# Attention then a two-layer block on one core: layer steps over 36 slots a batch, none in the slots that turn a k

## The chip, the cores and the metric

The kernel runs on one core of a Trainium2 chip. A core has a matrix engine (TensorE), three other compute engines (VectorE, ScalarE, GpSimd), and 16 DMA engines, which run side by side and are ordered by semaphores. TensorE writes into PSUM; the other engines bring results from there to SBUF. The metric is the device time in microseconds of one execution, the median of three runs for the kernel before. Less is better.

## The reference

Batched attention with a threshold (8 batches, 8 heads, 576 positions, 64 wide), whose output is the input of two layers with g = h - tanh(h) in between:

```python
scores = scale * np.matmul(q, k.transpose(0, 1, 3, 2))
thresh = np.max(scores, axis=-1, keepdims=True) - tau
scores = np.where(scores >= thresh, scores, -1000000000.0)
scores = scores - np.max(scores, axis=-1, keepdims=True)
attn = np.exp(scores)
attn = attn / (np.sum(attn, axis=-1, keepdims=True) + 1e-09)
x = np.matmul(attn, v)          # heads side by side: 4608 tokens x 512
h = x @ w_in                    # 512 x 2048
g = h - np.tanh(h)
return g @ w_out                # 2048 x 512
```

## The kernel before

The attention is cut into 32 pairs of heads (four a batch) of nine tiles of 128 queries each, 288 tiles in all. One program loop goes through **slots** s; slot s computes the scores of tile s + 8, the `Prelu` of tile s + 5, the `Exp` of tile s, the product with v of tile s - 2, and the preparation of later pairs. Tiles come in twos: z of two tiles is transposed together (by a DMA from pair 6 on, on TensorE before), so `Exp` and the product with v stand in every second slot. An instruction stream per engine follows the order of the loop, so what a slot contains on one engine is done in that order.

The pools (the number is how many buffers a tag has):

```python
    z_pool = pool("z", 4)
    zt_pool = pool("zt", 6)
    p_pool = pool("p", 3)
    o_pool = pool("o", 2)
    wt_pool = pool("wt", 4)
    g_pool = pool("g", 2)
    t_pool = pool("t", 3)
    y_pool = pool("y", 2)
    x_pool = pool("x", 2)
    ps_big = pool("ps_big", 2, space=PSUM)
    ps_o = pool("ps_o", 1, space=PSUM)
    ps_h = pool("ps_h", 2, space=PSUM)
    ps_y = pool("ps_y", 1, space=PSUM)
```

The scores of a tile: four matmuls, the main 512 columns and the other 64, once with k and once with kS, a copy of k whose halves are swapped. VectorE then scales and takes the row maximum in one instruction (L341):

```python
        else:
            lhs = qT[:, (5 * hh + t) * P : (5 * hh + t + 1) * P]
            for n, kk in enumerate((kT, kS)):
                for dst, src in ((main, MAIN[hh]), (rem, REM[hh])):
                    nc.tensor.matmul(
                        out=ps[:, dst], lhsT=lhs, rhs=kk[:, src],
                        start=(n == 0), stop=(n == 1),
                    )
        sc = sc_pool.tile([P, S], F32, name="sc")
        if kind(i) == "B":
            mx = mxs[i] = mxs.pop(i - 1)
        else:
            mx = mxs[i] = mx3[i // 2 % len(mx3)]
        c = int(kind(i) == "B")
        nc.vector.tensor_scalar(
            out=sc, in0=ps[:, lo : lo + S], scalar1=SC, scalar2=None,
            op0=ALU.mult, op1=ALU.max, accum_out=mx[:, c : c + 1],
        )
        scs[i] = sc
```

The `Prelu` on ScalarE (L368) makes z from it, with a DMA transpose (L375) behind each second one; `Exp` (L404) makes the weights pT, and nine matmuls (L425, L432) multiply them with v:

```python
        nc.scalar.activation(
            out=z, in_=sc, func=ACT.Prelu, bias=nb, scale=1.0, alpha=STEEP
        )
        if on_pe(i):
            zts[i] = zt
        elif kind(i) == "B":
            zts[i] = zt_pool.tile([P, TPP, P], BF16, name="zT")
            nc.sync.dma_start_transpose(out=zts[i], in_=zt)
...
        else:
            n += off
            pt = p_pool.tile([P, TPP * P], FP16, name="pT")
            nc.scalar.activation(
                out=pt[:, 0 : n * P], in_=zts.pop(i)[:, 0:n, :], func=ACT.Exp
            )
...
        nc.tensor.matmul(
            out=po[:, t - 1 : t + 1, :], lhsT=pt[:, 4 * P : 5 * P],
            rhs=vb[:, hh, 4:6, :], start=True, stop=False, skip_group_check=True,
        )
        for n in range(8):
            ab, c = divmod(n, 4)
            blk = 5 * ab + c
            nc.tensor.matmul(
                out=po[:, t - 1 + ab, :], lhsT=pt[:, blk * P : (blk + 1) * P],
                rhs=vb[:, hh, c, :], start=False, stop=(n == 7), skip_group_check=True,
            )
```

To **turn** a k: nine transposes on TensorE, a copy on VectorE (L263), and two on GpSimd for the swapped copy kS (L269). q is turned in the same way, or by a DMA:

```python
    def turn(p, t):
        hl = hls.pop((p, t))
        if t == "q" and q_by_dma(p):
            m = mats[p, t] = qk_pool.tile([P, W], FP16, name=f"{t}T", tag=t)
            nc.sync.dma_start_transpose(
                out=m.rearrange("p (c r) -> p c r", c=TPP),
                in_=hl.rearrange("p c a d -> p (c a d)"),
            )
            return
        ps = ps_big.tile([P, W], FP16, name=f"ps_{t}", tag="big")
        for c in range(TPP):
            turn_chunk(
                ps[:, c * P : (c + 1) * P], c, hl[:, c, :, :].rearrange("p a d -> p (a d)")
            )
        m = qk_pool.tile([P, W], FP16, name=f"{t}T", tag=t)
        nc.vector.tensor_copy(out=m, in_=ps)
        mats[p, t] = m
        if t == "k":
            sw = qk_pool.tile([P, W], FP16, name="kS", tag="ks")
            for lo, hi in ((0, D), (D, 0)):
                o, i = sw[lo : lo + D, :], m[hi : hi + D, :]
                nc.gpsimd.tensor_copy(out=o, in_=i)
            mats[p, "ks"] = sw
```

`emit_x` transposes a pair's attention output for the layers; it runs at the fourth or fifth slot of the next pair and takes its PSUM buffer from `ps_h`:

```python
    def emit_x(p):
        o = osb.pop(p)
        pf = ps_h.tile([P, 320], F32, name="psX", tag="h")
        ps = pf[:, 0:256].bitcast(BF16)
        for t in range(4):
            nc.tensor.matmul(
                out=ps[:, t * P : (t + 1) * P],
                lhsT=o[:, t, :, :].rearrange("p a d -> p (a d)"),
                rhs=ident_bf, is_transpose=True, start=True, stop=True,
            )

        nc.tensor.matmul(
            out=pf[:, 256:320], lhsT=o[:, 4, :, :].rearrange("p a d -> p (a d)"),
            rhs=fold, start=True, stop=True,
        )
        b = p // HPAIR
        if p % HPAIR == 0:
            xs[b] = x_pool.tile([P, DM_C, MB], BF16, name="xT")
        nc.vector.tensor_copy(out=xs[b][:, p % HPAIR, :], in_=ps[:, 0:512])
        nc.vector.tensor_copy(out=xR[:, p % HPAIR, b, :], in_=pf[:, 256:320])
```

A **layer step** is one of two: an h step (`hidden`, four matmuls of 512 columns, then `Tanh` on ScalarE and the subtraction on VectorE in the following slot), or a y step (a quarter of `project`, four matmuls of 512 columns; after four quarters VectorE copies y out and a DMA stores it):

```python
    def hidden(m, n, ps):
        if n == 0:
            gs[m] = g_pool.tile([P, DF_C, MB], BF16, name="g")
        for c in range(DM_C):
            nc.tensor.matmul(
                out=ps, lhsT=w_in_sb[:, c, n * P : (n + 1) * P],
                rhs=xs[m][:, c, :] if m < B else xR[:, c, :, :],
                start=(c == 0), stop=(c == DM_C - 1),
            )
        halves.append((m, n, ps))

    halves, ths = [], []

    def bend():
        while halves:
            m, n, ps = halves.pop(0)
            th = t_pool.tile([P, MB], F32, name="th")
            nc.scalar.activation(out=th, in_=ps, func=ACT.Tanh)
            ths.append((m, n, ps, th))

    def shrink():
        while ths:
            m, n, ps, th = ths.pop(0)
            nc.vector.scalar_tensor_tensor(
                out=gs[m][:, n, :], in0=th, scalar=-1.0, in1=ps,
                op0=ALU.mult, op1=ALU.add,
            )

    def project(m, ms, part, ps, last, cols=slice(0, d_model)):
        for n in range(4 * part, 4 * part + 4):
            nc.tensor.matmul(
                out=ps, lhsT=gs[m][:, n, ms * P : (ms + 1) * P],
                rhs=w_out_sb[:, n, cols], start=(n == 0), stop=(n == DF_C - 1),
            )
        if part == 3:
            nc_ = cols.stop - cols.start
            yo = y_pool.tile(
                [P, nc_], F32, name="yo", tag="yo" if nc_ == d_model else f"yo{int(last)}",
                bufs=2 if nc_ == d_model else 1,
            )
            if last:
                nc.scalar.copy(out=yo, in_=ps)
            else:
                nc.vector.tensor_copy(out=yo, in_=ps)
...
        def h_step(n):
            if tail and n % 2:
                ps = ps_big.tile([P, MB], F32, name="psHt", tag="big")
            else:
                ps = ps_h.tile([P, MB], F32, name="psH", tag="h")
            hidden(m, n, ps)

        def y_step(m, ms, part):
            if part == 0:

                odd = tail and (m, ms) > (B - 2, 1) and ms % 2 == 0
                pl, tag = (ps_o, "o") if odd else (ps_y, "y")
                ys[m, ms] = pl.tile([P, d_model], F32, name="psY", tag=tag), odd
            ps, odd = ys[m, ms]
            project(m, ms, part, ps, odd)
```

The steps of stage m are put in an order, h and y by turns; a y step needs the h steps that it reads. A middle stage has 16 h steps and 16 y steps (13 of the batch before, 3 of its own), the first stage 16 and 3:

```python
        now = quarters(m - 1)[EARLY(m - 1) :] if m > 0 else []
        if m < NMB - 1:
            now += quarters(m)[: EARLY(m)]
        else:
            now += quarters(m)[:12]
        n = 16 + len(now)


        ahead = n - max(0, EARLY(m) - 3) - LAST if m < NMB - 1 else n - 9 - LAST
        steps, at, i = [], [], 0

        def ready(y):
            last = 4 * y[2] + 3
            return y[0] < m or len(at) > (last if m else 15) and at[last] + 2 < i

        while now or len(at) < 16:
            if len(at) < 16 and (
                not now or not ready(now[0]) or len(at) * ahead <= i * 16
            ) and not (m == B - 1 and i < FIRST):
                steps.append(lambda a=len(at): h_step(a))
                at.append(i)
            elif ready(now[0]):
                steps.append(lambda y=now.pop(0): y_step(*y))
            else:
                steps.append(lambda: None)
            i += 1
```

Stage m runs beside the attention of batch m + 1. The slot in which the preparation of a pair falls is set in `plan`: `first` is the slot in which the pair's first scores are computed, `d` is how many slots earlier a step comes.

```python
    plan = {}
    for p in range(1, NPAIR):
        first = TPP * p - AHEAD
        for d, f in PREP[3 if p == 1 else 0 :]:
            d -= p == 1 and d in (3, 5)
            if d in (7, 8) and q_by_dma(p):
                d = d + 2
            if p in (2, 4):
                d = {8: 9, 7: 8, 5: 6}.get(d, d)
            elif d == 5 and p >= 5:
                d = 6 if p % 2 else 3
            plan.setdefault(first - d, []).append(lambda p=p, f=f: f(p))
        d = 7 if q_by_dma(p) else 3 - (p == 1 or p >= 5)
        d = 4 if p in (2, 4) else d
        plan.setdefault(first - d, []).append(lambda p=p: turn(p, "q"))
```

The loop, with the spreading of the layer steps. At slot j = 2 + LAG = 4 of a batch's first pair the steps of a stage are made, and `share` of them is due in each slot that follows:

```python
    for s in range(-AHEAD, NTILE + LAG + 3):
        p, j = divmod(max(s, 0), TPP)
        if 0 <= s < NTILE and j == 2 + LAG and p % HPAIR == 0 and p >= HPAIR:
            assert not todo
            todo = layers(stage, False)
            share = len(todo) / (HPAIR * TPP - 2 - LAG)
            done, stage = 0.0, stage + 1
        if s == NTILE:
            todo = layers(stage, True)
            share, done, stage = 1, 0.0, stage + 1
        if 0 <= s + AHEAD - 1 < NTILE:
            shift(s + AHEAD - 1)
        if 0 <= s + AHEAD < NTILE:
            scores(s + AHEAD)
        if s == 1 - AHEAD:
            for t in ("k", "q", "ks"):
                turn_first(t, 1)
        for i in kinks.pop(s, []):
            kink(i)
        bend()
        for i in wts.pop(s, []):
            weights(i)
        if 0 <= s < NTILE + FIRST:
            if todo:
                done += share
                if s < NTILE and j == TPP - 1 and p % HPAIR == HPAIR - 1:
                    done = 1e9
                while todo and done >= 1:
                    todo.pop(0)()
                    done -= 1
        if s == 0:
            nc.vector.tensor_tensor(
                out=fold, in0=ident_bf[:, 0:64], in1=ident_bf[:, 64:P], op=ALU.add
            )
        shrink()
        for store in stores[:-1]:
            store()
        del stores[:-1]
        for i in atts.pop(s, []):
            pp, jj = divmod(i, TPP)
            if i < NTILE:
                attend(i)
                odd = pp % 2
                if jj == 3 + odd:
                    norm(pp, 0)
                elif odd and jj in (0, 8):
                    norm(pp - (jj == 0), 1)
            if pp and jj == 1 + pp % 2:
                emit_x(pp - 1)
        for step in plan.pop(s, []):
            step()
```

Of the kernel before, what the change touches and what calls it, by code (L numbers as in the profile page):

```python
# [18 lines left out]
def kernel(  # L19
# [26 lines left out]
    HPAIR = H // 2  # L46
    NPAIR = B * HPAIR
# [4 lines left out]
    TPP = 9  # L52
    NTILE = NPAIR * TPP
# [9 lines left out]
    AHEAD = 8  # L63
    LDK = 16
    MASK = 5
    LAG = 2
# [177 lines left out]
    def q_by_dma(p):  # L244

        return p >= 2 * HPAIR and p % 4 != 0
# [25 lines left out]
    def turn_first(t, part):  # L272

        hl = hls[0, t[0]]
        c0, c1 = ((0, 5), (5, TPP))[part]
        pl, tag = (ps_y, "y") if t == "ks" else (ps_h, "h")
        ps = pl.tile([P, 5 * P], FP16, name=f"ps1_{t}", tag=tag)
        for c in range(c0, c1):
            o = ps[:, (c - c0) * P : (c - c0 + 1) * P]
            if t == "ks":  # L280
                for a in range(2):
                    turn_chunk(o[64 * a : 64 * a + 64, :], c, hl[:, c, 1 - a, :])
            else:
                turn_chunk(o, c, hl[:, c, :, :].rearrange("p a d -> p (a d)"))
        if part == 0:
            mats[0, t] = qk_pool.tile([P, W], FP16, name=f"{t}T", tag=t)
        dst, n = mats[0, t][:, c0 * P : c1 * P], (c1 - c0) * P
        if part == 1 or t == "q":
            nc.scalar.copy(out=dst, in_=ps[:, 0:n])
        else:  # L290
            nc.vector.tensor_copy(out=dst, in_=ps[:, 0:n])
# [16 lines left out]
    def scores(i):  # L308
        p, hh, t = place(i)
        qT, kT, kS = mats[p, "q"], mats[p, "k"], mats[p, "ks"]  # L310
        ps = ps_big.tile([P, 1024], F32, name="psS", tag="big")
        main, rem, lo = slice(0, 512), slice(512, 576), 0
        if kind(i) == "B":
            main, rem, lo = slice(512, 1024), slice(448, 512), 448
        if hh is None:
            qrem = REM
            if q_by_dma(p):
                qrem = (slice(512, 640, 2), slice(513, 640, 2))
            for n, kk in enumerate((kT, kS)):
                for dst, srcs in ((main, MAIN), (rem, REM)):  # L320
                    for hh in range(2):
                        nc.tensor.matmul(
                            out=ps[64 * hh : 64 * hh + 64, dst],
                            lhsT=qT[:, qrem[hh]], rhs=kk[:, srcs[hh]],
# [22 lines that stand above are left out]
    def shift(i):  # L347

        if kind(i) == "A":
            return  # L350
        mx = mxs.pop(i)
        nb = st_pool.tile([P, 9], F32, name="nb", tag="nb")
        nc.vector.tensor_scalar(  # L353
            out=nb.rearrange("p (a b) -> p a b", b=3)[:, :, 0:2],
            in0=mx.rearrange("p (a b) -> p a b", b=4)[:, :, 0:3],
            scalar1=-1.0, scalar2=tau, op0=ALU.mult, op1=ALU.add,
        )
        nbs[i - 1], nbs[i] = nb[:, 0:1], nb[:, 1:2]

    def kink(i):  # L360
        sc, nb = scs.pop(i), nbs.pop(i)
        if kind(i) == "B":
            zt = zs.pop(i - 1)
            z = zt[:, S:W]
        else:
            zt = zs[i] = z_pool.tile([P, W], BF16, name="z")
            z = zt[:, 0:S]
# [8 lines that stand above are left out]
# [131 lines left out]
# [14 lines that stand above are left out]
# [109 lines left out]
    def w_cast():  # L630
        flat, wt, i, cols = loaded.pop(0)
        nc.gpsimd.tensor_copy(out=flat[:, i * cols : (i + 1) * cols], in_=wt)
# [26 lines left out]
# [13 lines that stand above are left out]
# [16 lines left out]
    todo, stage = [], 0  # L688
# [4 lines left out]
            plan.setdefault(-AHEAD, []).extend(plan.pop(at))  # L693


    kinks, wts, atts = {}, {}, {}
    for i in range(NTILE + 3):
        at = i - 4 if i < HPAIR * TPP else i
# [4 lines left out]
    for s in range(-AHEAD, NTILE + LAG + 3):  # L703
        p, j = divmod(max(s, 0), TPP)
        if 0 <= s < NTILE and j == 2 + LAG and p % HPAIR == 0 and p >= HPAIR:
            assert not todo
            todo = layers(stage, False)
            share = len(todo) / (HPAIR * TPP - 2 - LAG)
            done, stage = 0.0, stage + 1
        if s == NTILE:  # L710
            todo = layers(stage, True)
# [11 lines that stand above are left out]
        for i in wts.pop(s, []):  # L723
            weights(i)
        if 0 <= s < NTILE + FIRST:
            if todo:
                done += share
                if s < NTILE and j == TPP - 1 and p % HPAIR == HPAIR - 1:
                    done = 1e9
                while todo and done >= 1:  # L730
                    todo.pop(0)()
# [22 lines that stand above are left out]
        if s + AHEAD in cast_when:  # L754
            w_cast()
        if s + AHEAD in load_when:
            w_load(next(pieces))
# [54 lines left out]
```

## Time and profile before

| what | value |
|---|---|
| time, median of three runs | 533.57 us (533.13 to 533.61) |
| span of the profiled execution | 532.0 us |
| busy: TensorE, VectorE, ScalarE, GpSimd | 96%, 79%, 82%, 55% |
| the eight batches of attention, from the first score reduction of tile 8 to that of tile 287 | 16.53 to 449.46 us |
| the tail: the rest of the layers | 449.46 to 532.0 us |
| DMA: transposes of z, from issue to landing | 3.5 us, 117 of them |

How to read it: a busy share is an average over the whole span. The kernel has a start, eight batches and a tail, so the batches are looked at one by one, by windows. A matmul's record lasts longer than the time after which the next one starts, because matmuls are pipelined, so that a difference of two starts says what a piece of work costs TensorE, and the length of one record does not. In a line of the timeline, the first number is the start, the second the length of what is merged in the line, and the count at the end says how many instructions are merged; square brackets give the idle time before it and what ended that. "L341" is line 341 of the kernel.

### The profile page before, as it was taken

The page shows a single profiled execution, that of the slowest core. Times are in us where ns is not written, and L with a number is a line of the kernel's source. Part 1 is how long each engine was busy: PE and PEld are TensorE (multiplying, and loading weights), DVE is VectorE, ACT ScalarE, POOL GpSimd, SP SyncE. Part 2 cuts the span into 40 slices and gives each one's busy share as a digit, 9 for nine tenths or more (in the row PEclk, how much of TensorE's full clock was granted, in tenths as well). Part 3 has the DMA queues.
Part 4 walks back from the last instruction along what each step waited for, and adds up shares of the span by engine and source line. Part 5 has one row for each costly group of instructions (what it writes and reads, how often), then busy time and mean ns, then how long its engine had stood idle before and what let it go on. Part 6 is the DMA issues. An engine that isn't in the chain of part 4 may idle for free.

```text
span 532.0 us, 12716 instructions
## 1 busy us (share of the span) xinstructions
PE 509.2 (96%) x4606; PEld 287.6 (54%) x4606; DVE 421.0 (79%) x1179; ACT 435.8 (82%) x617; POOL 290.1 (55%) x390
## 2 busy tenths in 40 slices
PE   8999899988999999999999999999999999999996
PEld 4666566544555555555555555555555555444444
DVE  5899879996888988898889988898889887554440
ACT  5999899988898989898898989898989899543330
POOL 8999989683746657475727574666657530000000
PEclk9999999998999999999999999999999999999999
DMA  7843659979897999789898899999979996400113
GB/s 212 252 133 114 217 186 184 167 160 197 170 209 140 190 184 217 173 179 202 186 197 186 191 188 199 171 185 199 214 160 185 195 149 110 105 33 28 39 41 80
DMA packets 208607, 86.79 MB, mean 163 GB/s; under 512 B 176160, under 2 KB 200992, under 8 KB 208544
## 3 DMA queue, kind: packets, MB, share of 16 engines
q1 hardware_dynamic: 207952, 85.56, 76.0%
q8 instruction: 36, 0.59, 0.5%
q10 hardware_dynamic: 592, 0.43, 0.3%
q14 instruction: 27, 0.22, 0.1%
HBM read 36.70 MB, written 9.44 MB: 87 GB/s over the span
## 4 chain that ended last, share of the span: by engine, by line
PE 35%; issue 20%; POOL 19%; ACT 9%; DMA 8%; DVE 6%; SPq 2%; POOLq 0%; ACTq 0%; DVEq 0%
PE psY L524 12%; PE psH L498 9%; PE psS L331 6%; POOL kS L269 5%; DMA vraw<-in_v_dram 4%; ACT z L368 3%; ACT pT L396 3%; PE psHt L498 3%; DMA kraw<-in_k_dram 3%; POOL khl L193 3%; POOL vb L221 2%; POOL qhl L193 2%; ACT th L511 1%; POOL qhl L192 1%; PE psO L432 1%
## 5 line engine op out<-in xcount | busy, mean ns | idle before, releaser
L341 DVE TENSOR_SCALAR_CACHE_REDUCE sc<-psS 128x576 f32<-128x576 f32 x288 | 214.2, 753 | 39.8 <-PE psS L331 25.9
L368 ACT ACTIVATE z<-sc,nb 128x576 bf16<-128x576 f32 x288 | 216.4, 772 | 22.2 <-DVE nb L353 20.3
L524 PE MATMUL psY<-w_out_sb,g 128*128 128x512 bf16 (+1 forms) x592 | 145.9, 373 | 0.8 <-DVE yo L537 0.8
L404 ACT ACTIVATE pT<-zT 128x1152 f16<-128x1152 bf16 x117 | 135.2, 1156 | 13.4 <-DMA zT<-z 13.2
L269 POOL COPY kS<-kT 64x1152 f16<-64x1152 f16 x62 | 70.9, 1144 | 125.9 <-DVE nb L353 124.4
L498 PE MATMUL psH<-xT,w_in_sb 128*128 128x512 bf16 x480 | 124.1, 381 | 2.6 <-DVE g L517 2.5
L331 PEld LDWEIGHTS <-qT 128*128 128x128 f16 x1024 | 74.8, 98 | 62.3 <-issue 8.4
L331 PE MATMUL psS<-kT,qT 128*128 128x512 f16 (+1 forms) x512 | 104.6, 286 | 3.2 <-DVE sc L341 1.2
L517 DVE SCALAR_TENSOR_TENSOR g<-th,psH 128x512 bf16<-128x512 f32 x128 | 87.6, 684 | 20.9 <-ACT th L511 20.4
L331 PE MATMUL psS<-kS,qT 128*128 128x512 f16 x496 | 101.6, 286 | 1.7 <-POOL kS L269 1.6
L511 ACT ACTIVATE th<-psH 128x512 f32<-128x512 f32 x128 | 74.8, 585 | 22.4 <-PE psH L498 21.8
L524 PEld LDWEIGHTS <-g 128*128 128x128 bf16 x592 | 51.0, 98 | 56.9 <-issue 2.4
L498 PEld LDWEIGHTS <-w_in_sb 128*128 128x128 bf16 x576 | 49.4, 98 | 57.9 <-issue 6.0
L432 PE MATMUL psO<-vb,pT 128*128 128x65 bf16 x1024 | 53.5, 194 | 0.0
L432 PEld LDWEIGHTS <-pT 128*128 128x128 f16 x1024 | 44.4, 98 | 9.7
L193 POOL TENSOR_TENSOR qhl<-qraw,qhl 128x576 f16<-128x576 f32 x31 | 39.7, 1281 | 2.6
L193 POOL TENSOR_TENSOR khl<-kraw,khl 128x576 f16<-128x576 f32 x31 | 39.7, 1281 | 2.6
L396 ACT ACTIVATE pT<-psZ 128x512 f16<-128x512 bf16 (+1 forms) x54 | 35.2, 655 | 3.9 <-PE psZ L387 3.5
L537 DVE COPY yo<-psY 128x512 f32<-128x512 f32 (+1 forms) x31 | 21.2, 682 | 14.1 <-PE psY L524 12.4
L425 PE MATMUL psO<-vb,pT 128*128 128x130 bf16 x128 | 28.3, 221 | 3.3 <-ACT pT L404 2.7
L458 DVE TENSOR_TENSOR osb<-psO,rc 128x256 bf16<-128x256 f32 x64 | 27.2, 424 | 2.2
L263 DVE COPY kT<-ps_k 128x1152 f16<-128x1152 f16 x31 | 23.3, 753 | 4.1 <-PE ps_k L240 4.1
(79 smaller groups left out, 508.8 us busy)
## 6 DMA issues: line engine op xcount, KB each, us to landing
vraw<-in_v_dram SPq DMA_DIRECT2D x32, 256.0 KB, 4.0
out_dram<-yo SPq DMA_DIRECT2D x32, 256.0 KB, 2.8
kraw<-in_k_dram SPq DMA_DIRECT2D x31, 256.0 KB, 3.2
qraw<-in_q_dram SPq DMA_DIRECT2D x31, 256.0 KB, 3.4
wt<-in_moe_w_in_dram SPq DMA_DIRECT2D x8, 512.0 KB, 4.6
wt<-in_moe_w_out_dram SPq DMA_DIRECT2D x8, 512.0 KB, 3.9
zT<-z SPq DMA_TRANSPOSE x117, 3.5
qraw<-in_q_dram SPq DMA_DIRECT2D x32, 32.0 KB, 3.3
```

The source lines that it names most:

```text
L193: nc.gpsimd.tensor_tensor(out=hl[:, :, 1, :], in0=x, in1=hl[:, :, 0, :], op=ALU.subtract)
L269: nc.gpsimd.tensor_copy(out=o, in_=i)
L331: nc.tensor.matmul(out=ps[:, dst], lhsT=lhs, rhs=kk[:, src], start=(n == 0), stop=(n == 1),)
L341: nc.vector.tensor_scalar(out=sc, in0=ps[:, lo : lo + S], scalar1=SC, scalar2=None, op0=ALU.mult, op1=ALU.max, accum_out=mx[:, c : c + 1],)
L368: nc.scalar.activation(out=z, in_=sc, func=ACT.Prelu, bias=nb, scale=1.0, alpha=STEEP)
L396: nc.scalar.activation(out=pt[:, off * P : (off + n) * P], in_=ps[:, 0 : n * P], func=ACT.Exp)
L404: nc.scalar.activation(out=pt[:, 0 : n * P], in_=zts.pop(i)[:, 0:n, :], func=ACT.Exp)
L432: nc.tensor.matmul(out=po[:, t - 1 + ab, :], lhsT=pt[:, blk * P : (blk + 1) * P], rhs=vb[:, hh, c, :], start=False, stop=(n == 7), skip_gr ...
L498: nc.tensor.matmul(out=ps, lhsT=w_in_sb[:, c, n * P : (n + 1) * P], rhs=xs[m][:, c, :] if m < B else xR[:, c, :, :], start=(c == 0), stop= ...
L511: nc.scalar.activation(out=th, in_=ps, func=ACT.Tanh)
L517: nc.vector.scalar_tensor_tensor(out=gs[m][:, n, :], in0=th, scalar=-1.0, in1=ps, op0=ALU.mult, op1=ALU.add,)
L524: nc.tensor.matmul(out=ps, lhsT=gs[m][:, n, ms * P : (ms + 1) * P], rhs=w_out_sb[:, n, cols], start=(n == 0), stop=(n == DF_C - 1),)
```

## The change

Only the list of slots that take a layer step is changed. Before, a stage's steps are spread evenly over the slots from j = 4 of the batch's first pair to the end of the batch: 32 slots, with none in the first four slots of the next batch. After, the room is the 36 slots from there to the slot before the next stage begins, so it reaches over the first four slots of the next batch, and the slots in which a k is turned on TensorE (`turns`) are taken out of it. `turns` repeats the rule by which `plan` places the turn of a k: six slots ahead for odd pairs, three for even ones, from pair 5 on. The last stage in the loop ends with the attention, and its room keeps all its slots. The purpose is to even out TensorE's work per slot: no slot without a layer step where no turn makes up for it, and no slot with both.

```diff
--- before.py
+++ after.py
@@ -693,6 +693,12 @@
             plan.setdefault(-AHEAD, []).extend(plan.pop(at))
 
 
+
+    turns = set()
+    for p in range(HPAIR + 1, NPAIR):
+        d = 6 if p % 2 else 3
+        turns.add(TPP * p - AHEAD - (d if p >= 5 else 5))
+
     kinks, wts, atts = {}, {}, {}
     for i in range(NTILE + 3):
         at = i - 4 if i < HPAIR * TPP else i
@@ -705,7 +711,10 @@
         if 0 <= s < NTILE and j == 2 + LAG and p % HPAIR == 0 and p >= HPAIR:
             assert not todo
             todo = layers(stage, False)
-            share = len(todo) / (HPAIR * TPP - 2 - LAG)
+            room = range(s, min(s + HPAIR * TPP, NTILE))
+            if room[-1] + 1 < NTILE:
+                room = [a for a in room if a not in turns]
+            share = len(todo) / len(room)
             done, stage = 0.0, stage + 1
         if s == NTILE:
             todo = layers(stage, True)
@@ -723,9 +732,9 @@
         for i in wts.pop(s, []):
             weights(i)
         if 0 <= s < NTILE + FIRST:
-            if todo:
+            if todo and (s >= NTILE or s in room):
                 done += share
-                if s < NTILE and j == TPP - 1 and p % HPAIR == HPAIR - 1:
+                if s < NTILE and s == room[-1]:
                     done = 1e9
                 while todo and done >= 1:
                     todo.pop(0)()
```

## The prediction

> **What bounds the kernel now.** I read the busy shares first, then a table by stage, then TensorE's own order of instructions in three places. The busy shares:
>
> ```profile
> PE 509.2 (96%) x4606; PEld 287.6 (54%) x4606; DVE 421.0 (79%) x1179; ACT 435.8 (82%) x617; POOL 290.1 (55%) x390
> ```
>
> TensorE is at the top, but its matmul records overlap and have modelled ends, so 96% doesn't say how full it is. For the stages I cut the span where the score reduction (VectorE, L341) of tile 8, 44, 80 and so on starts, which is where slots 0, 36, 72 begin. Batch m is then the 36 slots of attention of batch m, with the layers of batch m-1 beside it. Columns: stretch, length, busy time and instructions of TensorE, its weight load, VectorE, ScalarE and GpSimd, granted clock, DMA share, GB/s. Batches 0 to 7, then the tail:
>
> ```profile
> 16.53:60.90 44.37, 40.33 (x550) 28.29 (x546) 40.12 (x127) 41.97 (x68) 41.86 (x52) 1.00 0.56 166
> 60.90:116.54 55.64, 52.02 (x561) 32.47 (x560) 48.52 (x141) 52.06 (x79) 45.98 (x59) 1.00 0.79 180
> 116.54:177.49 60.95, 57.98 (x519) 32.26 (x517) 50.33 (x143) 52.10 (x71) 35.16 (x46) 0.97 0.91 180
> ...
> 292.86:350.31 57.45, 56.56 (x519) 31.69 (x517) 50.32 (x143) 52.11 (x71) 34.45 (x45) 1.00 0.96 189
> ...
> 407.52:449.46 41.94, 40.82 (x364) 22.25 (x361) 35.79 (x103) 38.55 (x53) 15.55 (x20) 1.00 0.88 158
> 449.46:532.00 82.54, 77.37 (x425) 37.39 (x423) 34.32 (x60) 32.08 (x51) 0.00 (x0) 0.99 0.21 56
> ```
>
> Batches 3 to 6 are alike (58.00, 57.37, 57.45, 57.21 us). Batch 2 is 3.5 us longer at a clock of 0.97. ScalarE has over 5 us of slack in a steady batch, VectorE 7; the DMA engines, at 0.96, have hardly any. To see whether TensorE has some, I went by its starts. The beginning of batch 5 in the timeline of TensorE (start, us, line, what, count):
>
> ```profile
> 293.24 0.23 PE L425 MATMUL psO<-vb,pT 128*128 128x130 bf16 x1
> ...
> 293.68 0.41 PE L331 MATMUL psS<-kT,qT 128*128 128x512 f16 x2
> ...
> 294.36 0.41 PE L331 MATMUL psS<-kT,qT 128*128 128x512 f16 x2
> ...
> 295.15 0.23 PE L425 MATMUL psO<-vb,pT 128*128 128x130 bf16 x1
> ...
> 295.73 0.41 PE L331 MATMUL psS<-kT,qT 128*128 128x512 f16 x2
> ...
> 296.22 1.03 PE L498 MATMUL psH<-xT,w_in_sb 128*128 128x512 bf16 x4
> 297.08 0.41 PE L331 MATMUL psS<-kT,qT 128*128 128x512 f16 x2
> ...
> 297.57 1.03 PE L524 MATMUL psY<-w_out_sb,g 128*128 128x512 bf16 x4
> 298.44 0.22 PE L425 MATMUL psO<-vb,pT 128*128 128x130 bf16 x1
> ...
> 298.75 0.41 PE L331 MATMUL psS<-kT,qT 128*128 128x512 f16 x2
> ```
>
> From start to start, where nothing waits: a layer step takes 0.86 to 0.87 us (296.22 to 297.08; 297.57 to 298.44), the scores of a tile 0.49 (297.08 to 297.57), an attend 0.31 (298.44 to 298.75). A turned k takes 0.51: in the timeline at slot 25 of batch 5 its nine transposes start at 332.37 and the next scores at 332.88. An x of four transposes and a fold is 0.25 (295.48 to 295.73).
>
> Now the batch. 36 x 0.49 + 32 x 0.865 + 18 x 0.31 + 4 turned k and 1 turned q x 0.51 + 4 x 0.25 = 17.6 + 27.7 + 5.6 + 2.6 + 1.0 = 54.5 us of 57.4. **TensorE bounds it**, with some 2.9 us not filled. Of that, the lull (slots 0 to 3, no layer step) holds this much: from 293.24 to 296.22 are 2.98 us, in which stand two attends, three scores and an x, 0.62 + 1.47 + 0.25 = 2.34. **0.64 us is idle.** The rest is spread: the shared tiles on half the array, a wait of 0.3 us at slot 9 on kS, one of 0.3 us at slot 21 on g.
>
> Batch 2 is different in its lull:
>
> ```profile
> 119.99 1.16 ACT L404 ACTIVATE pT<-zT 128x1152 f16<-128x1152 bf16 x1 [2.57 <-DMA zT<-z]
> 121.21 0.23 PE L425 MATMUL psO<-vb,pT 128*128 128x130 bf16 x1 [2.52 <-ACT pT L404]
> ...
> 123.09 1.85 PE L498 MATMUL psH<-xT,w_in_sb 128*128 128x512 bf16 x4
> ```
>
> ScalarE stood 2.57 us for a DMA transpose, TensorE 2.52 for ScalarE, and afterwards a layer step that elsewhere shows 1.03 shows 1.85: the clock had gone down.
>
> **What the Trainium skill says.** "Perfetto Trace Analysis", Identifying the Most-Contended Engine: matmul busy time is no measure of how full TensorE is. The trace agrees: 56.56 us of busy time in batch 5 stand against 54.5 by starts, so I reckon with starts. The same page, Optimization Strategy: where the most-contended engine changes over time, interleaving the regimes may help. That is this change, and the trace shows the two regimes, but the lull is only 3.86 us of a batch (292.86 to 296.72). "TensorE: Matmul & The Clock Gate", Wait — 56ns, not 53.3ns?: 512 columns are issued every 215.7 ns when warm, so a layer step is 0.863 us; the trace has 0.86 to 0.87. The same page, What's actually happening: an idle window of about 3.4 us halves the clock. Here a recorded stop of 2.52 us, with other short gaps around it, was enough.
>
> **The change, part by part.** It adds and removes no instruction. A middle stage has 32 steps (16 h, 16 y) and still has 32 slots for them: 36 in the room less four turns (slots 7, 13, 25 and 31 of the batch). So the share stays at one step a slot. Moved are four steps per stage, from the turn slots into slots 0 to 3 of the next batch. The first stage has 19 steps in 32 slots (share 0.594), of which three fall into the lull of batch 2, at its slots 0, 2 and 3. The last middle stage keeps its old 32 slots, turns included, and the tail of 82.54 us is as before. So lulls of six batches, 2 to 7, are filled.
>
> (1) Turn slots: the step's 0.865 us leaves a slot where TensorE was full (at slot 25 the chain step, attend, turn, scores runs without a gap). Each such slot gets shorter by that, 3.46 us a batch.
>
> (2) Lull: four steps are 3.46 us, of which 0.64 us is free room. The lull grows from 3.86 to about 6.7 us. VectorE was busy for 3.83 us of the 3.86 there; with two more shrinks of 0.68 it needs 5.2, ScalarE with two more tanh of 0.58 and its own two pairs (z, z, pT: 1.44 + 1.16 each) needs 6.4. Both fit, so TensorE sets the end.
>
> (3) Net per steady lull: -0.64 at best, in batches 3 to 7: -3.2 us. I count half, -1.6. For now h steps stand beside the x at slot 3, and both take ps_h buffers, of which there are two; slot 21, also an x slot, already shows a psH wait of 0.3 us. And with four slots skipped the h steps fall on odd slots for part of the batch, where tanh then meets another order of z and pT.
>
> (4) Batch 2: the three y steps come out of batch 1 (55.64 us, not dense on TensorE: 19 steps and 6 or so us unfilled) and give TensorE 2.6 us of work before and inside the stop. At best the stop of 2.5 us and the slow clock (3% of 61 us = 1.7) go: -4.2. The stop depends on where the v load and three transposes stand in the DMA queue, so I count half: -2.1, and +0.6 for what batch 1 loses in order.
>
> Sum: -1.6 - 2.1 + 0.6 = -3.1, so 533.6 - 3.1 = **530.5 us**.
>
> **Rivals.** (A) *The DMA takes over.* At a share of 0.96 a batch of 57.4 us holds 55 us of transfers, so a batch can't go much below that however TensorE is packed. For it: ScalarE's waits for zT (8.4 us over batches 3 to 6). Against: those waits hardly reach TensorE (psO on pT: 0.2 us over the same). If it is the bound, the gain is near zero: 533 us. (B) *The turns were no cost, and the lull was a needed rest.* In the lull ScalarE has 5.2 us of z and pT for 3.86 us of span and works off its backlog later; the DMA queue too. If filling it makes shrinks late, VectorE's reductions come late and with them scores: a few tenths a batch lost, 535 us. For it: VectorE has only 0.03 us spare in the lull. Against: with the lull at 6.7 us it has 1.5. (C) *The whole of the idle time is got,* batch 2's stop and clock included, and steady turns flow better: -3.2 - 4.2 = 526 us.
>
> **Range and chances.** The floor by TensorE is 54.5 a batch; a gain of over 2%, 10.7 us, would need nearly all idle time of batches 2 to 7, and nothing moved acts on most of it. A loss of that size needs a new stop of over 1.7 us in each of six batches. So 526.5 to 535 in 8 of 10; faster by over 2% 0.03, within 0.95, slower 0.02.
>
> **What would show it.** Batches 3 to 6 at 56.5 to 57.3 us each, batch 2 at 57 to 60 with a clock nearer 1.00, the tail the same within 0.5 us. TensorE's starts in the lull with a psH or psY in each of slots 0 to 3 and no gap; slots 7, 13, 25 and 31 without one. Wrong would be: a steady batch over 58 us, with waits of psH on g or psX on g at slots 3 and 4, or a stop of psO on pT in any batch, or batch 2 unchanged at 61.

## The result, and the profile after

The changed kernel takes **533.11 us** (median of four runs, 532.01 to 533.36) against 533.35 us before: a ratio of 0.9986, with a 95% interval of 0.9969 to 1.0004. Nothing that can be measured was won. The prediction had said 530.5 us; its range, 526.5 to 535, holds the result, but the gain of 3 us that it gave reasons for is not there. By the page after, the engines are as busy as before (TensorE 96%, VectorE 79%, ScalarE 82%, GpSimd 54%).

The table by stage shows that the small sum hides larger parts. Batches 1, 2, 5, 7 and the tail, columns as before:

```profile
60.83:115.66 54.83, 50.56 (x547) 31.45 (x544) 48.51 (x140) 51.65 (x79) 46.33 (x60) 1.00 0.81 185
115.66:173.67 58.01, 55.92 (x512) 31.18 (x512) 49.32 (x144) 50.32 (x68) 35.06 (x45) 1.00 0.99 183
...
289.17:347.40 58.23, 57.08 (x518) 31.69 (x517) 50.54 (x146) 51.60 (x71) 34.34 (x45) 1.00 0.95 185
...
405.12:448.92 43.80, 43.43 (x379) 23.46 (x378) 37.02 (x108) 40.08 (x56) 15.03 (x20) 1.00 0.82 156
448.92:531.40 82.48, 77.36 (x425) 37.39 (x423) 34.31 (x60) 32.02 (x51) 0.00 (x0) 0.99 0.20 56
```

Batch 2 went from 60.95 to 58.01 us and its clock from 0.97 to 1.00. Batches 3 to 6 took 230.03 us before and take 231.45 now: **0.36 us more each**, where 0.3 less was expected. Steps have moved between batches (a step is 0.865 us), and for these the table's cut is not even: it lies at a reduction, which at batch 2 starts 0.82 us after slot 0's first scores before the change and 1.46 us after them now, so that a step of slot 0 falls to batch 1. Cut at the first scores of slot 0 instead, batch 1 goes from 55.63 to 54.18 us with three steps less (2.60 us), so it lost 1.1; batch 2 goes from 61.05 to 58.45 with one less, so it won 1.7; batch 7, from its slot 0 to its slot 27, goes from 41.98 to 44.13 with four more (3.46), so it won 1.3.

The lull is filled as planned. TensorE's timeline at the start of batch 5 (slots 2 and 3):

```profile
292.02 1.03 PE L498 MATMUL psH<-xT,w_in_sb 128*128 128x512 bf16 x4
292.89 0.41 PE L331 MATMUL psS<-kT,qT 128*128 128x512 f16 x2
...
293.38 1.03 PE L524 MATMUL psY<-w_out_sb,g 128*128 128x512 bf16 x4
294.24 0.22 PE L425 MATMUL psO<-vb,pT 128*128 128x130 bf16 x1
```

A step in each slot and every start at the end of the work before it: 292.89 less 292.02 is 0.87, 294.24 less 293.38 is 0.86. Slots 0 to 3 take 6.65 us in place of 3.60 (from the scores of slot 0 to those of slot 4, mean of batches 3 to 6), 3.06 more for 3.46 us of steps: 0.41 us was won there, and lost elsewhere. The waits of TensorE in batches 3 to 6 (us in total, times, longest) tell where. Before, then after:

```profile
PE psS L331 <- POOL kS L269: 1.3, 4, 0.3
PE psH L498 <- DVE g L517: 1.3, 4, 0.3
PE psO L425 <- ACT pT L404: 0.2, 1, 0.2
```

```profile
PE ps_k L240 <- DVE sc L341: 1.4, 8, 0.2
PE psS L331 <- POOL kS L269: 1.3, 4, 0.3
PE psS L331 <- DVE sc L341: 0.4, 1, 0.4
```

The waits of psH on g in slot 22, behind the x of slot 21, are gone, the one on kS stays, and a new one has come, eight times in four batches: the **turn of a k waits for a score reduction on VectorE**. TensorE's timeline around slot 25 before the change, from its scores to those behind the turned q:

```profile
330.71 0.41 PE L331 MATMUL psS<-kT,qT 128*128 128x512 f16 x2
...
332.37 0.67 PE L240 MATMUL ps_k<-ident_f,khl 128*128 128x128 f16 x9
332.88 0.41 PE L331 MATMUL psS<-kT,qT 128*128 128x512 f16 x2
...
334.73 0.41 PE L331 MATMUL psS<-kT,qT 128*128 128x512 f16 x2
```

The changed kernel around the same slot, now a turn without a step:

```profile
328.43 0.41 PE L331 MATMUL psS<-kT,qT 128*128 128x512 f16 x2
...
328.78 0.75 DVE L341 TENSOR_SCALAR_CACHE_REDUCE sc<-psS 128x576 f32<-128x576 f32 x1
328.94 0.22 PE L425 MATMUL psO<-vb,pT 128*128 128x130 bf16 x1
...
329.45 0.76 DVE L341 TENSOR_SCALAR_CACHE_REDUCE sc<-psS 128x576 f32<-128x576 f32 x1
329.59 0.66 PE L240 MATMUL ps_k<-ident_f,khl 128*128 128x128 f16 x9 [0.18 <-DVE sc L341]
...
330.27 0.41 PE L331 MATMUL psS<-kT,qT 128*128 128x512 f16 x2
...
332.40 0.41 PE L331 MATMUL psS<-kT,qT 128*128 128x512 f16 x2
```

The attend starts at 328.94 and lasts 0.31, so TensorE is ready to turn at 329.25. The turn needs a `ps_big` buffer; of the two, one holds the scores just written and the other those of the tile before, which VectorE reads from 328.78 until about 329.5. The turn starts at 329.59, the nine transposes (0.51) are through at 330.10, and then the next scores wait for the second reduction and start at 330.27. Before the change the stretch was 330.71 to 334.73, 4.02 us; now it is 328.43 to 332.40, 3.97 us. **Taking 0.865 us of work out of slot 25 saved 0.05 us.** (The list of waits shows less than that: it has 0.18 us for the turn at 329.59, because a matmul's record ends later than the next one could start; by starts it is 329.59 less 329.25, 0.34.)

In slot 7 the stretch from its scores to the next, before and after:

```profile
300.10 0.41 PE L331 MATMUL psS<-kT,qT 128*128 128x512 f16 x2
...
302.29 0.41 PE L331 MATMUL psS<-kT,qT 128*128 128x512 f16 x2
```

```profile
299.18 0.41 PE L331 MATMUL psS<-kT,qT 128*128 128x512 f16 x2
...
301.02 0.41 PE L331 MATMUL psS<-kT,qT 128*128 128x512 f16 x2
```

That is 2.19 and 1.84: 0.35 us saved of 0.865.

The same reckoning by starts over all slots, as means of batches 3 to 6, closes the sum. The lull's four slots grew by 3.06 us, slots 21 and 22 fell by 0.48, and the four turn slots, each with the slot behind it, fell by 0.41 (7), 0.89 (13), 0.05 (25) and 0.86 us (31): together 2.2 in place of 3.46. So the two turns of odd pairs gave the step's time in full, and the two of even pairs gave 0.46 of 1.73.

### The profile page after: what moved, and what is told of

Read it like the earlier page. It is cut to its first block, busy times and chain, and to the rows that moved or that the text cites. A ratio compares the mean times of both kernels' runs of the same rounds, so it can differ in the third digit from the quotient of the medians.

```text
span 531.4 us, 12707 instructions
## 1 busy us (share of the span) xinstructions
PE 509.7 (96%) x4606; PEld 286.3 (54%) x4606; DVE 421.6 (79%) x1179; ACT 433.3 (82%) x617; POOL 289.4 (54%) x390
## 4 chain that ended last, share of the span: by engine, by line
PE 51%; issue 13%; DVE 11%; ACT 11%; POOL 7%; DMA 6%; SPq 1%; ACTq 0%; POOLq 0%; DVEq 0%
PE psY L524 16%; PE psH L498 13%; PE psS L331 10%; ACT z L368 4%; DVE sc L341 4%; ACT pT L396 3%; DMA zT<-z 3%; PE psO L432 3%; PE psHt L498 3%; POOL kS L269 2%; PE psS L322 2%; DVE g L517 2%; ACT th L511 2%; ACT pT L404 2%; DMA kraw<-in_k_dram 2%
## 5 line engine op out<-in xcount | busy, mean ns | idle before, releaser
L387 PE MATMUL psZ<-ident_bf,z 128*128 128x128 bf16 x243 | 22.6, 220 | 2.3 <-ACT pT L396 1.3
```

## The experiments

The theory (T): a turn without a step beside it makes TensorE wait for VectorE through `ps_big`, at slots 7 and 25 above all, and this eats what the lull gives. Rivals: the DMA engines, at a share of 0.95 to 1.00, set the length of a batch (D); or it is the new order of h and y steps, with h on odd slots (P). All edits are against the changed kernel. The lengths come from the table by stage, cut at reductions, so that where the lull of batch 2 is filled, most of its first step counts with batch 1; "gaps" are the slots from 4 on, counted over the stage, that take no step. Each ratio is to runs of the kernel before on the same chip.

| kernel | gaps | batch 1 | batch 2 | mean of 3 to 6 | batch 7 | time | ratio to before (95%) |
|---|---|---|---|---|---|---|---|
| before | 0 to 3 | 55.64 | 60.95 | 57.51 | 41.94 | 533.35 | |
| changed | 7, 13, 25, 31 | 54.83 | 58.01 | 57.86 | 43.80 | 533.11 | 0.9986 (0.9969 to 1.0004) |
| all 36 | 4, 12, 21, 30 | 55.58 | 58.72 | 56.42 | 43.81 | 528.52 | 0.9896 (0.9862 to 0.9929) |
| lull left empty | 7, 13, 25, 31 and 0 to 3 | 55.96 | 61.38 | 59.72 | 41.54 | 543.62 | 1.0184 (1.0141 to 1.0227) |
| odd turns out | 4, 13, 21, 31 | 55.23 | 58.06 | 56.31 | 43.81 | 527.53 | 0.9883 (0.9841 to 0.9924) |
| even turns out | 4, 7, 21, 25 | 54.65 | 58.96 | 57.69 | 43.81 | 533.75 | 1.0000 (0.9986 to 1.0014) |
| even turns earlier | 7, 13, 25, 31 | 54.83 | 58.50 | 58.19 | 44.18 | 535.42 | 1.0044 (1.0028 to 1.0060) |
| y copy on ScalarE | 7, 13, 25, 31 | 55.27 | 57.52 | 57.16 | 43.61 | 531.69 | 0.9970 (0.9957 to 0.9983) |
| first stage alone | 0 to 3 from batch 3 on | 54.82 | 59.34 | 57.79 | 41.34 | 531.10 | 0.9955 (0.9940 to 0.9971) |
| no v from pair 12 | 7, 13, 25, 31 | 54.82 | 56.95 | 57.79 | 43.87 | 531.61 | one run |
| x slots out | 3, 13, 21, 31 | 57.71 | 55.20 | 56.97 | 43.23 | 528.70 | 0.9904 (0.9875 to 0.9933) |
| odd out, y on ScalarE | 4, 13, 21, 31 | 55.23 | 58.61 | 56.24 | 43.61 | 527.38 | 0.9880 (0.9860 to 0.9900) |
| odd out, again | 4, 13, 21, 31 | 55.24 | 58.85 | 56.45 | 43.81 | 529.21 | 0.9915 (0.9894 to 0.9936) |
| away from turns and norms | 4, 17, 21, 35 | 54.14 | 58.38 | 56.30 | 43.50 | 527.11 | 0.9885 (0.9859 to 0.9910) |

**All 36 slots take steps.**

```diff
-        turns.add(TPP * p - AHEAD - (d if p >= 5 else 5))
+        pass
```

> All 36 slots of the room take steps, turns too, 32 steps in them: the four gaps fall at slots 4, 12, 21 and 30, so all k turns keep a step beside them. Theory T (the changed kernel loses in the turns of slots 7 and 25 what it gains in the lull: without a step, TensorE is there before VectorE has read the scores whose PSUM buffer the turn needs, 1.2 us a batch): that wait goes and the lull stays filled, so batches 3 to 6 come to 56.2 to 56.8 us each (changed kernel 57.7 to 58.2) and the time to 527 to 530 us. Rival D (the DMA engines, at a share of 0.95 to 1.00, set the length of a batch): 57.4 to 58.2 us a batch as before and after, 532.5 to 534 us. Rival P (the h steps on odd slots are what costs): the gaps still move h to odd slots for half of the batch, so 57.5 or more, 532 to 534 us.

Measured: 528.52 us, 56.10 to 56.74 us a steady batch. With the lull filled and all turns beside a step, 1.1 us a batch goes against before. Half of the change is good. The waits on the reduction are not all gone: two are left in batches 3 to 6, up to 0.7 us, at slot 7 of batch 4 and slot 13 of batch 6, though a step stands beside both turns.

**The other half alone: turns without a step, lull empty.**

```diff
-            room = range(s, min(s + HPAIR * TPP, NTILE))
+            room = range(s, min(s + HPAIR * TPP - 4, NTILE))
```

> The other half of the change alone: no steps in the turn slots 7, 13, 25, 31, but the lull stays empty too, so four of the other slots (12, 20, 28, 35) take two steps. Theory T: the waits at slots 7 and 25 come (1.2 us a batch) and the lull's idle 0.6 stays: batches 3 to 6 at 58 to 59 us, batch 2 near 61 to 62, the time 536 to 541 us. Rival D: 57.4 to 58 us a batch, 533 to 535. Rival P: the same h order as in the changed kernel for a part, so about 57.8 and 534 to 536.

Measured: 543.62 us, 59.46 to 60.47 a batch, more than T had said. Of TensorE's waits in batches 3 to 6, these three are on VectorE's reading of `ps_big`:

```profile
PE psS L331 <- DVE sc L341: 2.5, 4, 0.6
PE psS L331 <- DVE kT L263: 1.4, 4, 0.3
...
PE ps_k L240 <- DVE sc L341: 0.7, 4, 0.2
```

The four slots with two steps, which this run had to bring in, got longer by the step alone (slot 12 takes 2.21 us in place of 1.35). The loss of 2.2 us a batch is in the turn slots, which with the slots behind them gave only 1.75 of 3.46, and in slots 0 to 3, which grew by 0.52. Whether the second steps made VectorE later at these places, the run doesn't tell.

**Only odd, or only even turns without a step.** Both have four gaps, two of them at 4 and 21.

```diff
+        if p % 2:          # odd; "== 0" for even
             turns.add(TPP * p - AHEAD - (d if p >= 5 else 5))
```

> Only the turns of odd pairs (slots 13, 31) are taken out; the other two gaps fall at slots 4 and 21. Theory T: at slots 13 and 31 the turn stands behind an x and shared attends, which give VectorE time, and no wait is made there; batches 3 to 6 at 56.2 to 56.8 us, 527 to 530 us, as with all 36. Rival D: 57.4 to 58.2, 532.5 to 534. Rival P: 57.5 or more, 532 to 534.

> Only the turns of even pairs (slots 7, 25) are taken out; the other two gaps fall at slots 4 and 21. Theory T: the 1.2 us of waits at slots 7 and 25 are as in the changed kernel, so batches 3 to 6 at 57.4 to 58.2 us and 532 to 534.5 us, 4 to 5 us above the kernel that takes out the odd ones. Rivals D and P: no difference between taking out the odd or the even ones over 1 us.

Measured: 527.53 and 533.75 us, 56.31 and 57.69 a batch. Same number of steps, of gaps, of filled lulls; the one difference, gaps at 13 and 31 or at 7 and 25, is 1.4 us a batch. By starts, slots 13 and 31 without a step take 1.97 and 1.85 us, with one 2.71 before the change; slots 7 and 25 without a step take 2.22 each, as much as with one (2.18 and 2.17 before). In the kernel with the even turns out TensorE's first wait is the one that T names, twice a batch:

```profile
PE psS L331 <- DVE sc L341: 6.0, 8, 0.8
```

P falls with this: the faster of the two has eight h steps on odd slots of a batch, the slower two. D falls too: the kernel with the odd turns out moves the same data in 56.31 us.

**Even turns two slots earlier, gaps kept.**

```diff
-                d = 6 if p % 2 else 3
+                d = 6 if p % 2 else 5
```

(in `plan` only)

> The changed kernel with its gaps where they are (slots 7, 13, 25, 31), but the k of even pairs turned two slots earlier, at slots 5 and 23, beside a step. Theory T (what costs is the turn in a gap, since it needs a score buffer that VectorE has not read yet): a gap without a turn costs nothing, as the gaps at 4, 12, 21 and 30 of the all-36 kernel did, and kS is ready in time at slot 9 (0.5 us), so batches 3 to 6 at 56.1 to 56.6 us and 526.5 to 529.5 us. Rival G (these slots can't be gaps, turn or no turn, because the norm and the y copy before them make VectorE late): the waits at slots 6 to 8 and 24 to 26 stay at 0.5 us or more each, 57.0 us or more a batch, 530.5 to 532.5 us.

Neither came: 535.42 us. The waits in batches 3 to 6, the first two:

```profile
PE psS L331 <- DVE kT L263: 3.4, 8, 0.4
PE psS L331 <- DVE sc L341: 3.0, 3, 1.3
```

At slots 7 and 25, now gaps without a turn, TensorE's starts follow without a stop (0.80 us, an attend and the scores): a gap alone is free there, as T said. But at slots 5 and 23, where the turn went, the y copy and a norm stand in VectorE's queue ahead of the copy of kT, and scores wait for that copy although there is a step beside (slots 6 and 24 take 1.94 us in place of 1.35). And three batches got a stop of about 1 us behind the turn of slot 13. So T was too narrow: what costs is a turn that finds VectorE late, and the step beside it is only one way to give VectorE time.

**VectorE relieved of the y copy.**

```diff
-            if last:
+            if last or m < B - 2:
                 nc.scalar.copy(out=yo, in_=ps)
```

> The changed kernel with the copy of y out of PSUM (0.69 us, four a batch) on ScalarE in place of VectorE for the batches in the loop. It stands two slots ahead of the turns of slots 7 and 25. Theory T: VectorE is earlier by up to 0.69 us there, so the waits of ps_k and psS on the score reduction at those slots fall from 1.2 us a batch to 0.6 or less, batches 3 to 6 at 56.9 to 57.4 us, 528.5 to 531.5 us. Rival L (the wait is the fixed round trip of two buffers, reduction then copy, and not VectorE's queue): no change, 57.7 to 58.2 us and 532.5 to 534 us, or longer if ScalarE takes its own time for it.

Measured: 531.69 us, just above what T had said, with 56.91 to 57.51 a batch, three of the four in what it had said. The waits in batches 3 to 6, first and last of the list:

```profile
PE psS L331 <- POOL kS L269: 1.0, 4, 0.2
...
PE psS L331 <- DVE sc L341: 0.2, 1, 0.2
```

The wait of the turn on the reduction is gone from the list. With the gaps unchanged, an earlier VectorE takes 0.7 us of a batch away, 0.33 in each of slots 7 and 25 (1.84 to 1.51 us); the fixed round trip of two buffers (L) can't be the cause of that part. Something is left: 1.51 is 0.2 more than the scores, attend and turn of such a slot (0.49, 0.31 and 0.51), and slot 26 takes 2.14 us as in the changed kernel, where it took 1.86 before. Whether that rest is the round trip is open; a third `ps_big` buffer was not tried.

**The first stage alone.**

```diff
-            room = range(s, min(s + HPAIR * TPP, NTILE))
-            if room[-1] + 1 < NTILE:
+            room = range(s, min(s + HPAIR * TPP - 4 * (p > HPAIR), NTILE))
+            if p == HPAIR:
```

> The change in the first stage alone: its 19 steps go over the 36 slots less four turns, so three y steps come into the lull of batch 2; all other stages as before the change. If the stop of 2.5 us in the lull of batch 2 and the slow clock behind it are ended by the three steps: no stop over 1 us in batch 2, its clock at 1.00, batch 2 at 58 to 60 us in place of 60.95 (it now has three steps more than before), batch 1 at 54.8, batches 3 to 6 at 57.2 to 58 as before, in all 530 to 532 us. If the stop is a matter of the DMA queue and not of the lull's pace: batch 2 at 61 us or more, 533 to 535 us.

Measured: 531.10 us. The stop and the slow clock are gone (the clock of batch 2 is 1.00, the longest wait that is listed 0.3 us). From slot 0's scores on, batch 2 takes 60.08 us with three steps more (2.60 us) than before, when it took 61.05: 3.6 us won. In its slots 0 to 4 alone it is 4.5 us, and some of that is lost again at the turns behind. Batch 1, with three steps less, fell from 55.63 to 54.17 us where its work fell by 2.60: 1.1 us lost.

**No loads and casts of v from pair 12 on** (this kernel computes with old v, and its time is that of less work).

```diff
+        if t == "v" and p >= 12:
+            return
```

(and the same in `split_v`)

> The changed kernel without the loads and casts of v from pair 12 on (it goes on with older v, so it leaves out a third of the plain loads and a part of GpSimd's work). Rival D (the DMA engines set a batch's length): batches 3 to 6 shorter by 1 us or more. Theory T: the waits at the turns of slots 7 and 25 stay, 57.4 to 57.8 us a batch, at most the 0.5 us of kS at slot 9 less.

Measured in one run: 57.76 to 57.86 a steady batch, against 57.72 to 58.23 with v. DMA share 0.90 to 0.94 in place of 0.95 to 1.00, and three of the four steady batches as long as with v (batch 5 is 0.46 us shorter, D had said 1 or more for each): D is out for these. Batch 2 is 1.06 us shorter; the wait of 1.3 us that it has in the changed kernel did not come here, and one run doesn't tell why. The wait on kS did not fall.

**Gaps at the x slots, and the odd turns out with the y copy on ScalarE, and the odd turns out again.**

```diff
-        turns.add(TPP * p - AHEAD - (d if p >= 5 else 5))
+        turns.add(TPP * p - AHEAD - (6 if p % 2 else 7))      # x slots
```

> Four gaps again taken out of the 36 slots, but at slots 3, 13, 21 and 31, the slots of the x transposes, and none with an even turn. Theory T: no wait is made, TensorE full in steady batches, 56.0 to 56.6 us each and 526.5 to 529 us, as for the kernel with gaps at 4, 13, 21, 31. If it were the taking out of slots as such that costs: 57.5 us and 532 to 534.

> The kernel that takes out only the odd turns (gaps 4, 13, 21, 31), with the y copy on ScalarE besides. Theory T: there TensorE is full already (about 55.0 us of work and 1.0 us of the shared tiles' own), so an easier VectorE brings nothing: batches 3 to 6 at 56.0 to 56.6, 526.5 to 528.5 us. If VectorE were the bound behind it, 1 us or more a batch would go, 522 to 524 us.

> The kernel that takes out only the odd turns, once more with more rounds, as the version that beats both: 0.985 to 0.991 of the time before, 526.5 to 528.5 us.

Measured: 528.70, 527.38 and 529.21 us. The x slots gave 56.68 to 57.54 a batch, above what T had said, with stops behind the turn of slot 13, a gap there too. Its batch 1 is the longest of all: behind the turn of slot 31 TensorE waits 1.3 us for a reduction, and 3.41 us at half the clock follow. The repeat has one batch of 57.27 beside 56.10, 56.10 and 56.34, with the same kind of stop, and its time is a little above what was expected. With the y copy on ScalarE too, all four are 56.05 to 56.49. T had said that this brings nothing; on the same chip its five times (527.11 to 527.63) all lie below the six of the repeat (527.87 to 530.44), though they overlap with the first run of the kernel without it, on another chip (527.49 to 528.58). So T's "nothing" is not shown.

**Four gaps away from turns and norms.**

```diff
-    for p in range(HPAIR + 1, NPAIR):
-        d = 6 if p % 2 else 3
-        turns.add(TPP * p - AHEAD - (d if p >= 5 else 5))
+    for b in range(1, B):
+        turns.update(HPAIR * TPP * b + a for a in (4, 17, 21, 35))
```

> The 36 slots less four that are away from every turn and every norm (slots 4, 17, 21 and 35): all turns, odd ones too, have a step beside them. Theory T, as widened by the run with gaps at the x slots (a turn in a gap, at slot 13 too, makes TensorE stand for VectorE in some batches, up to 1.3 us): no such stop, batches 3 to 6 at 56.0 to 56.3 us, all alike, 525.5 to 527.5 us. If the stops at slot 13 have another cause: batches of 56.1 to 57.5 us, unlike each other, 527.5 to 529.5 us as the kernels with gaps at 12 or 13.

Measured: 527.11 us, 0.9885 of before, batches of 56.45, 56.28, 56.10 and 56.36, none with a stop, though a little over what was expected. All that is listed of TensorE's waits in batches 3 to 6:

```profile
PE psS L322 <- DVE sc L341: 0.2, 1, 0.2
```

This version beats both kernels, by 6 us; the one with the odd turns out is as good within the intervals. In batch 2 it still has two stops of 1.1 us behind the turns of slots 7 and 25 (3.25 us each in place of 2.17), with a step beside them; why there stays open.

## Why the prediction failed

1. **The bound** was right. TensorE sets the pace: where little makes it wait, a batch takes 56.1 us (not the 54.5 of the prediction's sum), and moving steps into idle time shortens it.
2. **The lull** was right in mechanism. 0.64 us of idle time at most, five times, was the estimate, of which half was counted. It was filled without a stop, also at the x of slot 3, where a wait had been feared. It gave 0.41 us a batch: the idle time is gone, but a step between the scores of two shared tiles, in slots 0 and 1 (576 queries are four and a half tiles, so a pair's two heads share one), takes longer than 0.865 us (from 288.77 to the scores at 289.74 in batch 5, 0.97). The wait behind the x of slot 21 went away too, 0.48 us. The kernel with all 36 slots, 1.1 us a batch shorter than before, has both, and 0.36 us of slots 9 and 10, where the wait on kS is gone. (That wait is in slot 10 and the one on g in slot 22, counted by the scores; the prediction has 9 and 21.)
3. **The turn slots were the step that failed.** "Each such slot gets shorter by that, 3.46 us a batch" was taken from TensorE running without a gap at slot 25. But there the step gave VectorE 0.865 us to read the scores. Without it slot 25 with the slot behind it got shorter by 0.05 us and slot 7 with its next by 0.41; slots 13 and 31 gave 0.89 and 0.86. That is 2.2 of the 3.46 us, 1.25 a batch too little, more than the lull and slot 22 together brought (0.41 and 0.48). The slot that the prediction had looked at gave the least. I had read off TensorE's queue alone what its freed time would be worth, and had not asked what would be waited for next. In the list of rivals, B looked for VectorE's lateness in the lull, where it did not come, and called the turns by name only in its heading.
4. **Batch 2** was right in mechanism. The stop and the slow clock go whole, as the first stage alone shows: 4.5 us in slots 0 to 4, where 4.2 at best had been put down, and 3.6 over the batch. (The prediction's 1.7 us for the slow clock is 3.41 us at half of it; 3% of 61 would be 1.8.) In the changed kernel 1.7 us of that is left, near the 2.1 that were counted; its list of waits has a psS on the reduction of 1.3 us, behind the turn of slot 13. Batch 1 lost 1.1 us in both, about twice the 0.6 put down.
5. **The DMA rival** described the result (533 us) for a wrong reason. The share of 0.96 was no bound: at 0.98 to 1.01 the kernel with the odd turns out has batches shorter by 1.2 us than before.

## What to carry to other kernels

A slot in which an engine is full need not be a slot in which it can be relieved: ask what it would wait for if its work there were gone, and read from the other engine's queue when that would be ready. Where two users share a two-buffer pool, filler between them isn't waste, since it covers the reader's time; put gaps where the reader is idle. A change with two halves is best run as two kernels: here the filled lull with a step beside every turn was worth -1%, and the gaps at two of the four turns undid it.

## What the runs showed of the hardware

The mean DMA share reached 1.01 to 1.03 in stretches of 56 us while those batches got shorter, so a share near 1 was not the mark of a bound here. A stop of 2.52 us on TensorE was followed by the slow clock (a layer step's record of 1.85 us in place of 1.03), and so was one of 1.30 us, in batch 1 of the kernel with gaps at the x slots; each time the clock was at half for 3.41 us. A stop of 1.3 us in batch 2 of the changed kernel was not followed by it, so its length alone doesn't decide. And in several of the traces 68 of 4606 matmul records are missing, x4538 on the page of the kernel with the odd turns out, all of them of layer steps; for each a start is left out, a hole of 216 ns, and some of these holes stand in the list of waits as a wait on "issue", which is none.
